# Dense matmuls issued in four 32-column tiles, and down weights loaded in the middle of the first GLU

## Chip, cores, metric

One core of one Trainium2 chip. The metric is the device time of one execution in microseconds; lower is better. Unless said otherwise, fast runs are compared with fast runs taken on the same chip in the same rounds. A "ratio" is the mean time of one kernel's fast runs over the mean of the other's fast runs of the same rounds, so it is not quite the ratio of the medians quoted beside it.

## The reference, cut

```python
def _A_ref(x, wqkv, wo):             # B=1, S=2048, D=640
    H = 32; Dh = 20; W = 256         # sliding window of 256 keys
    q, k, v = split_heads(x @ wqkv)
    scores = q k^T * Dh ** -0.5      # masked: 0 <= query - key < W
    p = softmax(scores)
    return merge_heads(p v) @ wo

def _B_ref(x, w_gate, w_up, w_down): # F=1536
    return (sigmoid(x @ w_gate) * (x @ w_up)) @ w_down

xn = layernorm(x)
return x + _A_ref(xn, wqkv, wo) + _B_ref(xn, w_gate, w_up, w_down)
```

All tensors are bf16.

## The kernel before

The sequence is cut into four chunks of 512 rows. A list of attention steps drives the order of TensorE's work: each of 76 steps computes scores, and two steps after a head group's last scores its PV (the product p v) follows (32 times). Between steps a queue of dense work ("fill": the GLU, which is `_B_ref` without its last product, projections, output) is emitted so that TensorE never waits for the exponential. All of it is unrolled: every matmul is an instruction pair, a weight load and a matmul (the trace of the kernel before has 4,666 loads and 4,631 matmuls).

```python
def proj_block(w, c, m):                       # q and k
    ...
        nc.tensor.matmul(ps, lhsT=wt[:, m, :], rhs=xnT[c][:, d, :],
                         start=(d == 0), stop=(d == DC - 1))        # 128x128 tile, 512 columns

def g_gu(c, f0, f1):                           # GLU, gate and up: the same form, 512 columns
def project_v / down / add_wo                  # the same form, 320 columns

def scores(c, step):
    ...                                        # four heads, 20 rows each, 64 columns: 20*64 tiles
        nc.tensor.matmul(ps[hf * U:(hf + 1) * U, i, ...],
                         lhsT=qk["k", kc][32 * i:32 * i + DH, g, key:key + U], rhs=qk["q", c][...])
def pv(c, g, parts):
    ...                                        # four heads side by side: 128*32 tiles
        nc.tensor.matmul(acc[32 * i:32 * i + 32, ...], lhsT=v[:, h * VW:h * VW + 32], rhs=pt[:, i, ...])

# the order of the steps
for t, (c, k, step) in enumerate(todo):
    ...
    for group in [x for x in ends if ends[x] == t - 2]:
        pv(*group, parts.pop(group))           # dense -> PV
    made = (step, scores(c, step))             # PV or dense -> scores
    ...
    credit = fill.pull(credit)                 # scores -> dense
```

q and k go through a scratch in DRAM to be spread over partitions; each chunk from the second on reads back 1 MB of q and 1 MB of k (in two pieces).

## Time and profile before

| | before |
|---|---|
| time, median (lowest to highest) | 315.97 us (315.47 to 316.91), 4 runs |
| TensorE instructions in the program | 9,334 |
| TensorE (PE) busy | 98% of the span, clock 1.0 |
| next busiest engine | ScalarE, 61% |
| drains (stops of TensorE at a change of tile size, about 95 ns each from the last tile's end) | 185, about 19.6 us |

PE is the bound; the prediction below shows the lines and how they are read. One line also belongs here. This is the queue on which PE's own instructions arrive (packets, MB, share of 16 engines' span):

```profile
q8 instruction: 36, 0.59, 0.8%
```

36 packets of 16 KB in 314 us: with 9,334 instructions of PE that is some 259 a packet.

### The profile page before, as it was taken

The page shows a single profiled execution, that of the slowest core. Times are in us where ns is not written, and L with a number is a line of the kernel's source. Part 1 is how long each engine was busy: PE and PEld are TensorE (multiplying, and loading weights), DVE is VectorE, ACT ScalarE, POOL GpSimd, SP SyncE. Part 2 cuts the span into 40 slices and gives each one's busy share as a digit, 9 for nine tenths or more (in the row PEclk, how much of TensorE's full clock was granted, in tenths as well). Part 3 has the DMA queues.
Part 4 walks back from the last instruction along what each step waited for, and adds up shares of the span by engine and source line. Part 5 has one row for each costly group of instructions (what it writes and reads, how often), then busy time and mean ns, then how long its engine had stood idle before and what let it go on. Part 6 is the DMA issues. An engine that isn't in the chain of part 4 may idle for free.

```text
span 314.3 us, 10536 instructions
## 1 busy us (share of the span) xinstructions
PE 306.9 (98%) x4631; PEld 176.7 (56%) x4666; DVE 157.3 (50%) x313; ACT 193.2 (61%) x179; POOL 159.8 (51%) x257
## 2 busy tenths in 40 slices
PE   8999999999999999999999999999999999999996
PEld 3654444456566656544566656544456664444674
DVE  3531486654855553447943542454552433673234
ACT  5723786788754468676644558776765657777200
POOL 3000487676768447454955536355355655565300
PEclk9999999999999999999999999999999999999999
DMA  7996976935823155500045025600000010000002
GB/s 237 376 319 195 322 189 121 369 139 187 225 59 70 41 180 190 172 4 0 2 47 85 23 103 154 205 3 2 3 2 23 23 44 2 4 2 2 1 2 83
DMA packets 34573, 33.08 MB, mean 105 GB/s; under 512 B 9920, under 2 KB 33984, under 8 KB 34496
## 3 DMA queue, kind: packets, MB, share of 16 engines
q1 hardware_dynamic: 34096, 32.14, 34.1%
q8 instruction: 36, 0.59, 0.8%
q10 hardware_dynamic: 432, 0.28, 0.3%
q14 instruction: 9, 0.07, 0.1%
HBM read 21.00 MB, written 10.26 MB: 99 GB/s over the span
## 4 chain that ended last, share of the span: by engine, by line
PE 85%; DMA 8%; SPq 2%; ACT 2%; issue 1%; DVE 0%; ACTq 0%
PE y L413 14%; PE pu L399 14%; PE pqk L292 13%; PE pg L392 13%; PE ps L459 7%; PE acc L491 7%; PE y L420 6%; PE pv L318 5%; DMA wu<-in_B_w_up_dram 4%; DMA sk<-st 3%; DMA wo<-wo_i 2%; PE pwarm L236 2%; PE d L413 2%; SPq L221 1%; ACT pT L464 1%
## 5 line engine op out<-in xcount | busy, mean ns | idle before, releaser
L467 POOL TENSOR_SCALAR_AFFINE_SELECT pT<-pT 128x512 bf16<-128x512 bf16 (+2 forms) x192 | 145.5, 789 | 132.8 <-ACT pT L464 132.7
L464 ACT ACTIVATE pT<-ps 128x2048 bf16<-128x2048 f32 x76 | 142.7, 1878 | 63.3 <-PE ps L459 60.5
L403 DVE SCALAR_TENSOR_TENSOR h<-th,pu 128x512 bf16<-128x512 f32 x48 | 32.9, 685 | 53.8 <-PE pu L399 29.2
L392 PE MATMUL pg<-xnT,wg 128*128 128x512 bf16 x226 | 58.9, 380 | 0.7
L399 PE MATMUL pu<-xnT,wu 128*128 128x512 bf16 x228 | 58.0, 380 | 1.3 <-issue 0.6
L413 PE MATMUL y<-wd,h 128*128 128x320 bf16 (+1 forms) x348 | 50.2, 297 | 0.0
L292 PE MATMUL pqk<-xnT,wqkv 128*128 128x512 bf16 x191 | 45.6, 381 | 0.5
L413 PEld LDWEIGHTS <-h 128*128 128x128 bf16 x396 | 36.7, 98 | 14.3
L501 DVE STREAM_TRANSPOSE t<-acc 128x512 f32<-128x512 f32 x32 | 22.8, 713 | 34.6 <-PE acc L491 34.3
L395 ACT ACTIVATE th<-pg 128x512 f32<-128x512 f32 x48 | 28.6, 595 | 17.8 <-PE pg L392 13.3
L399 PEld LDWEIGHTS <-wu 128*128 128x128 bf16 x240 | 22.0, 98 | 25.8 <-issue 0.6
L392 PEld LDWEIGHTS <-wg 128*128 128x128 bf16 x240 | 22.0, 98 | 25.1 <-issue 0.2
L459 PE MATMUL ps<-qT,kT 20*64 20x128 bf16 (+4 forms) x1856 | 32.5, 239 | 0.4 <-ACT pT L464 0.2
L292 PEld LDWEIGHTS <-wqkv 128*128 128x128 bf16 x200 | 22.5, 119 | 18.0 <-issue 0.6
L459 PEld LDWEIGHTS <-kT 20*64 20x64 bf16 x1856 | 20.7, 103 | 19.3 <-issue 16.0
L424 DVE SCALAR_TENSOR_TENSOR xn<-y,xc 128x320 bf16<-128x320 f32 (+1 forms) x29 | 13.9, 483 | 29.8 <-PE y L420 29.8
L491 PEld LDWEIGHTS <-v 128*32 128x32 bf16 x1376 | 19.5, 97 | 13.6 <-issue 11.0
L491 PE MATMUL acc<-pT,v 128*32 128x64 bf16 (+3 forms) x1376 | 26.0, 223 | 0.0
L318 PE MATMUL pv<-wqkv,xnT 128*128 128x320 bf16 x160 | 23.8, 300 | 0.2 <-DVE xnT L273 0.2
L513 DVE TENSOR_TENSOR on<-t,rec 128x320 bf16<-128x320 f32 (+4 forms) x48 | 22.2, 463 | 1.1
L420 PE MATMUL y<-wo,oc 128*128 128x320 bf16 (+1 forms) x145 | 21.6, 297 | 0.3 <-DMA wo<-wo_i 0.3
L296 DVE CAST st<-pqk 128x512 bf16<-128x512 f32 x20 | 13.7, 690 | 12.3 <-PE pqk L292 11.4
(49 smaller groups left out, 153.6 us busy)
## 6 DMA issues: line engine op xcount, KB each, us to landing
qT<-sq SPq DMA_DIRECT2D x3, 1024.0 KB, 6.0
sq<-st SPq DMA_DIRECT2D x20, 128.0 KB, 3.4
sk<-st SPq DMA_DIRECT2D x20, 128.0 KB, 4.2
out_dram<-xn SPq DMA_DIRECT2D x15, 160.0 KB, 1.8
kT<-sk SPq DMA_DIRECT2D x3, 768.0 KB, 5.7
wg<-in_B_w_gate_dram SPq DMA_DIRECT2D x2, 960.0 KB
wu<-in_B_w_up_dram SPq DMA_DIRECT2D x2, 960.0 KB, 11.3
xc<-in_A_x_dram SPq DMA_DIRECT2D x3, 640.0 KB, 5.0
```

The source lines that it names most:

```text
L292: nc.tensor.matmul(ps, lhsT=wt[:, m, :], rhs=xnT[c][:, d, :], start=(d == 0), stop=(d == DC - 1))
L318: nc.tensor.matmul(ps[:, 0:HALF], lhsT=xnT[c][:, d, s * P:(s + 1) * P], rhs=wqkv[:, d, 2 * D + hf * HALF:2 * D + (hf + 1) * HALF], start=( ...
L392: nc.tensor.matmul(pg, lhsT=part(wg, d, f), rhs=xnT[c][:, d, :], start=(d == 0), stop=(d == DC - 1))
L395: nc.scalar.activation(out=th, in_=pg, func=TANH, scale=0.5)
L399: nc.tensor.matmul(pu, lhsT=part(wu, d, f), rhs=xnT[c][:, d, :], start=(d == 0), stop=(d == DC - 1))
L403: nc.vector.scalar_tensor_tensor(out=h, in0=th, scalar=1.0, in1=pu, op0=ADD, op1=MULT)
L413: nc.tensor.matmul(y[:, 0:cut[1] - cut[0]], lhsT=ht[c, f][:, s * P:(s + 1) * P], rhs=wd[:, f, cut[0]:cut[1]], start=(f == 0), stop=False)
L420: nc.tensor.matmul(y[:, 0:cut[1] - cut[0]], lhsT=oc[c, m][:, s * P:(s + 1) * P], rhs=wo[:, m, cut[0]:cut[1]], start=False, stop=(m == DC - 1))
L459: nc.tensor.matmul(ps[hf * U:(hf + 1) * U, i, col * U:(col + n) * U], lhsT=qk["k", kc][32 * i:32 * i + DH, g, key:key + U], rhs=qk["q", c] ...
L464: nc.scalar.activation(out=pt[:, :, 0:CW], in_=ps, func=EXP, scale=SCALE)
L467: nc.gpsimd.affine_select(out=out, in_=in_, pattern=[[0, HG], [0, n], [sign, width]], compare_op=GE, fill=0.0, base=base, channel_multipli ...
L491: nc.tensor.matmul(acc[32 * i:32 * i + 32, q * U:(q + n) * U], lhsT=v[:, h * VW:h * VW + 32], rhs=pt[:, i, col * U:(col + n) * U], start=( ...
```

## The change

Its intent: PV works in 128*32 tiles, dense work in 128*128, and each change of tile size costs one of these drains of about 95 ns. If dense work uses 128*32 too, the drain between dense work and PV falls away. The down weights are loaded earlier, while the DMA engines have room.

```diff
+    def dense(out, lhsT, rhs, start, stop):
+        for j in range(0, P, 32):
+            nc.tensor.matmul(out[j:j + 32], lhsT=lhsT[:, j:j + 32], rhs=rhs, start=start, stop=stop)
...
-            nc.tensor.matmul(ps, lhsT=wt[:, m, :], rhs=xnT[c][:, d, :],
-                             start=(d == 0), stop=(d == DC - 1))
+            dense(ps, wt[:, m, :], xnT[c][:, d, :], d == 0, d == DC - 1)
 (the same for gate, up, down, wo, and for v of chunks 1 to 3)
...
-    fill.add("gu0", mix(g_gu(0, 0, 12), g_norms(1, True), 9), 12 * GU)
+    fill.add("gu0a", g_gu(0, 0, 4), 4 * GU)
+    fill.add("wd", later(load_wd), 0)
+    fill.add("gu0b", mix(g_gu(0, 4, 12), g_norms(1, True), 1), 8 * GU)
     fill.add("x2", later(load_x, 2), 0)
-    fill.add("wd", later(load_wd), 0)
```

More of the change, by code (lines that the diff above doesn't have):

```diff
@@ L317, in project_v @@
         for d in range(DC):
-            nc.tensor.matmul(ps[:, 0:HALF], lhsT=xnT[c][:, d, s * P:(s + 1) * P],
-                             rhs=wqkv[:, d, 2 * D + hf * HALF:2 * D + (hf + 1) * HALF],
-                             start=(d == 0), stop=(d == DC - 1))
+            (dense if c else nc.tensor.matmul)(
+                ps[:, 0:HALF], lhsT=xnT[c][:, d, s * P:(s + 1) * P],
+                rhs=wqkv[:, d, 2 * D + hf * HALF:2 * D + (hf + 1) * HALF],
+                start=(d == 0), stop=(d == DC - 1))
         return ps
@@ L391, in g_gu @@
             for d in range(DC):
-                nc.tensor.matmul(pg, lhsT=part(wg, d, f), rhs=xnT[c][:, d, :],
-                                 start=(d == 0), stop=(d == DC - 1))
+                dense(pg, part(wg, d, f), xnT[c][:, d, :], d == 0, d == DC - 1)
             th = tp.tile([P, CW], FP32, name="th")
@@ L398, in g_gu @@
             for d in range(DC):
-                nc.tensor.matmul(pu, lhsT=part(wu, d, f), rhs=xnT[c][:, d, :],
-                                 start=(d == 0), stop=(d == DC - 1))
+                dense(pu, part(wu, d, f), xnT[c][:, d, :], d == 0, d == DC - 1)
             h = hp.tile([P, CW], BF16, name="h")
@@ L412, in down @@
         for f in range(FC):
-            nc.tensor.matmul(y[:, 0:cut[1] - cut[0]], lhsT=ht[c, f][:, s * P:(s + 1) * P],
-                             rhs=wd[:, f, cut[0]:cut[1]], start=(f == 0), stop=False)
+            dense(y[:, 0:cut[1] - cut[0]], ht[c, f][:, s * P:(s + 1) * P],
+                  wd[:, f, cut[0]:cut[1]], f == 0, False)
             if f % 6 == 5:
@@ L419, in add_wo @@
         for m in range(DC):
-            nc.tensor.matmul(y[:, 0:cut[1] - cut[0]], lhsT=oc[c, m][:, s * P:(s + 1) * P],
-                             rhs=wo[:, m, cut[0]:cut[1]], start=False, stop=(m == DC - 1))
+            dense(y[:, 0:cut[1] - cut[0]], oc[c, m][:, s * P:(s + 1) * P],
+                  wo[:, m, cut[0]:cut[1]], False, m == DC - 1)
     def add_x(c, s, y, cut, rows):
```

## The prediction

> **What bounds the kernel now.** I read the page first, for the engine that sets the span.
>
> ```profile
> span 314.3 us, 10536 instructions
> PE 306.9 (98%) x4631; PEld 176.7 (56%) x4666; DVE 157.3 (50%) x313; ACT 193.2 (61%) x179; POOL 159.8 (51%) x257
> PEclk9999999999999999999999999999999999999999
> PE 85%; DMA 8%; SPq 2%; ACT 2%; issue 1%; DVE 0%; ACTq 0%
> ```
>
> TensorE matmuls (PE) cover 98% of the span at full clock, and PE makes up 85% of the chain that ended last; no other engine is above 61%. A matmul's recorded end is modelled, so 98% could still hide gaps. I therefore went to the PE's timeline and compared starts. This is one stretch of it, in the first output stage (start, length, what):
>
> ```profile
> 91.52 0.43 PE L459 MATMUL ps<-qT,kT 20*64 20x320 bf16 x24
> 91.88 2.62 PE L413 MATMUL y<-wd,h 128*128 128x320 bf16 x18
> 94.43 0.85 PE L491 MATMUL acc<-pT,v 128*32 128x320 bf16 x48
> 95.21 0.43 PE L459 MATMUL ps<-qT,kT 20*64 20x320 bf16 x24
> 95.57 1.53 PE L420 MATMUL y<-wo,oc 128*128 128x320 bf16 x10
> ```
>
> Three tile sizes alternate: 128*128 (dense), 128*32 (PV), 20*64 (scores, in 32-row by 64-column tiles). Inside a stretch there is no gap: 18 down matmuls are 2.62 us, the last one's modelled length is 0.30, so 17 spacings are 2.32 us, 136.5 ns each. At a change of size there is one. The last down matmul starts at 91.88 + 2.62 - 0.30 = 94.20 and should occupy the array to 94.34; PV begins at 94.43. Going through all starts of the trace in this way, with (columns / 2.4 + 3) ns for what a matmul or a set of concurrent tiles occupies (2.4 columns per ns is what 136 ns for 320 and 216 ns for 512 columns give), I find:
> - dense to PV: 32 changes, 96 ns each, 3.07 us in all;
> - PV to dense: 1 change, 108 ns;
> - dense to scores: 45 changes, 96 ns;
> - PV to scores: 31 changes, 107 ns;
> - scores to dense: 76 changes, 116 ns.
> The differences are the skew inside a concurrent set: its last tile starts about 12 ns (four PV tiles) or 23 ns (eight score tiles) after its first. Each change is then about 95 ns from the last tile. The sum is near 19.6 us. The first matmul after a change takes about 10 ns more than the next ones (146 against 136 ns). Outside the changes the remaining real stalls are few: some tenths of a us at 41.7, where PE waits for the second up weights, and at 89.25, where it waits for wo.
>
> ```profile
> 41.73 1.03 PE L399 MATMUL pu<-xnT,wu 128*128 128x512 bf16 x4 [0.32 <-DMA wu<-in_B_w_up_dram]
> 89.25 1.52 PE L420 MATMUL y<-wo,oc 128*128 128x320 bf16 x10 [0.25 <-DMA wo<-wo_i]
> ```
>
> So PE is bound by columns streamed plus changes of tile size. Only a change in those two, or a new wait, moves the time.
>
> [...] in the groups below a PV weight load takes 97 ns, as a dense one does (98), and it hides even under 64-column sets that start 28 ns apart.
>
> ```profile
> L491 PEld LDWEIGHTS <-v 128*32 128x32 bf16 x1376 | 19.5, 97 | 13.6 <-issue 11.0 <-DVE mv L250 0.4 <-DVE st L296 0.4
> L413 PEld LDWEIGHTS <-h 128*128 128x128 bf16 x396 | 36.7, 98 | 14.3
> L292 PEld LDWEIGHTS <-wqkv 128*128 128x128 bf16 x200 | 22.5, 119 | 18.0 <-issue 0.6
> ```
>
> [...] 2,000 successive PE instructions (1,000 load and matmul pairs) begin within 51.2 us, 51 ns a pair.
> [...] The trace shows the blocks (36 of them on the PE's instruction queue, about 1 us each)[...].
>
> **The change, part by part.**
> *Dense in four column tiles.* All gate, up, q, k, down and wo matmuls, and V of chunks 1 to 3, become four 128*32 ones with the same moving operand. The instruction lists agree: 17,500 PE rows against 9,334, so 8,166 more, which is 1,361 dense matmuls x 3 extra x 2 (load and matmul). Columns streamed stay the same if the four run side by side, as in PV: a 320-column PV set at 94.715 is followed by the next at 94.851, 136 ns, exactly a dense 320's. So the stream costs nothing more.
> - Removed: 32 dense-to-PV drains, 32 x 96 = 3.07 us; one PV-to-dense, 0.11; the slow first set after them, 32 x 10 = 0.32. Sum -3.50 us, all on PE, all on the path.
> - Added: before a score step the last dense set is now skewed by 11 ns, 45 x 11 = 0.50 us; one new change between the untiled V of chunk 0 and the q projection, 0.10 us. Sum +0.60.
> - Unchanged: the 76 changes into scores and the 76 out of them, since scores keep their own size. Some 16.4 of the 19.6 us of drains stay.
> Net -2.9 us, 0.9%.
>
> *Down weights earlier.* In the program's order the load now stands after four of twelve GLU blocks. It waits for no engine, so the queue issues it right behind the clears of the scratch, near 37.5 us in place of 52.4:
>
> ```profile
> 36.93 0.60 SPq L191 DMA_DIRECT2D sk<-kT  x1
> 44.77 6.92 SPq L276 DMA_TRANSPOSE xnT<-xn  x4
> 51.74 0.58 SPq L155 DMA_DIRECT2D xc<-in_A_x_dram  x1
> 52.38 0.63 SPq L212 DMA_DIRECT2D wd<-in_B_w_down_dram  x1
> ```
>
> The windows view tells what it meets: DMA share 0.99 from 36 to 43 us, 0.13 from 43 to 46, 0.84 from 46 to 53 (the transposes), 1.02 from 53 to 61 (x and wd). The load is 1.97 MB, at the 345 GB/s of the last window 5.7 us. It fills 43 to about 48.7, the idle stretch and the start of the transposes, which then end near 56 and not 53.7. The next projection needs them all at 56.9. So it is hidden, with under 1 us to spare; I allow +0.2 us. What it frees (the q stores that stood behind it at 60 to 66 us) was not on PE's path; gain 0. wd itself is first read near 82 us and was never late.
> A little of the gain may be lost at 89 us, where the wait for wo grows if PE arrives sooner: +0.1.
>
> Sum: 315.8 - 2.9 + 0.3 = 313.2 us.
>
> **The rivals.**
> 1. *Dispatch becomes the bound.* Dense 320-column work will need 8 instructions per 136 ns, 17 ns each, and the whole program averages about 300 us / 17,500 = 17 ns. PV and score bursts need 7 ns (144 instructions in 1.03 us)[...]. Against: PV and score bursts show no stall at their end[...]. So it is harmless or plainly harmful, with little between: about 318 to 325 us if it bites.
> 2. *Four column tiles don't stream side by side for dense operands.* All four read one moving operand, where PV's four read different ones, and the q and k weights are strided (119 ns a load against 98). For: no dense case is in the trace. Against: PV reads four streams at full rate, and 216 ns per 512-column set leaves room for loads. If the q and k sets alone lost 10%, that is 200 x 22 ns = 4.3 us, and the time 317.
> 3. *The early load collides.* If the transposes end after 57 us, PE waits at the first projection; at most the 2 to 3 us that they slip less the margin, so 314 to 315 us.
> 4. *The change saves more*, since dense to scores also gets cheaper between column-tiled sizes. Against: PV to scores costs 107 ns now, both column-tiled, no less than dense to scores.
>
> **Range and chances.** The arithmetic of the drains is firm to about 0.5 us: 312.6 to 313.6 if nothing else occurs. Rival 3 and a mild form of 1 or 2 stretch that to 317. A strong form of rival 1 gets 14%: slower by over 2% means above 322.1. Faster by over 2% means below 309.5, which would need another 3.7 us, more than the drains removed hold: 3%. I predict 313.2 us, 312.0 to 317.0 in eight of ten, 0.03 faster, 0.83 same, 0.14 slower.
>
> **What would show it.** Right: in the PE's timeline PV follows dense work without a gap (starts one set apart), the matmul sets of 320 and 512 columns keep 136 and 216 ns, changes into and out of scores keep 107 and 116 ns, and the GLU's first projection near 57 us shows no DMA wait. Rival 1: gaps of PE with "issue" as their reason, or sets that start more than 136 ns apart, most in the output stages and V, where sets have 320 columns, and least in the GLU. Rival 2: longer spacing at all shapes or at q and k only, GLU included. Rival 3: a wait of the q projection on the transposed xnT. I am wrong if the drain remains between dense and PV although both have 128*32, or if the 320-column sets come out above 140 ns in the output stages.

## The result, and the profile after

The changed kernel took 325.99 us (324.14 to 327.44, 4 runs) against 315.97: ratio 1.031, 95% interval 1.0247 to 1.0374. The fast runs of a second set on another occasion (after_again below) gave 1.031 too. It is slower by about 3%; the prediction was 313.2 us.

The page of the changed kernel, to be held against the first lines of the prediction and the instruction queue above:

```profile
span 325.0 us, 18737 instructions
PE 310.6 (96%) x8749; PEld 195.3 (60%) x8749; DVE 158.2 (49%) x313; ACT 193.4 (60%) x179; POOL 159.3 (49%) x257
PEclk9999999899999999999999999999999999999999
q8 instruction: 68, 1.11, 1.4%
```

PE is busy for 96% and no longer 98%, of a longer span; one slice shows a lower clock; and 68 blocks of instructions had to be fetched where 36 were (17,500 instructions in place of 9,334). No other engine became busier.

The intended effect is there. PE's timeline of the changed kernel around one PV (start, length, what, idle before and its end):

```profile
88.76 1.25 PE L284 MATMUL pu<-xnT,wu 128*32 128x512 bf16 x20
89.84 0.64 PE L494 MATMUL acc<-pT,v 128*32 128x320 bf16 x24
91.61 0.21 PE L494 MATMUL acc<-pT,v 128*32 128x64 bf16 x4 [1.13 <-issue]
91.76 0.43 PE L462 MATMUL ps<-qT,kT 20*64 20x320 bf16 x24
```

Five up sets of 216 ns begin at 88.76 and end at 89.84, and PV begins at 89.84: the drain is gone. Going through all starts, sets of four tiles keep the spacing of one dense matmul (about 3 ns over columns / 2.4: 136 ns for 320 columns, 216 for 512), changes into scores take 106 ns and out of scores 114 ns, as predicted. Set against the same sums of the kernel before, drains and first sets are 3.5 us less.

But the same lines show what came in: PV stops in the middle for 1.13 us, waiting for nothing that the profile knows ("issue"). In the table of waits of the changed kernel (engine, line, waited for: us in total, times, longest):

```profile
PE pv L284 <- issue: 2.9, 2, 2.1
PE pu L284 <- issue: 2.0, 1, 2.0
PE ps L462 <- DMA kT<-sk: 1.7, 1, 1.7
PE acc L494 <- issue: 1.1, 1, 1.1
```

I then listed every place after 14 us where a matmul starts over 60 ns later than the one before it and a drain explain, with the number of the instruction in PE's stream:

| start of the gap, us | gap, us | (instruction + 64) / 256 |
|---|---|---|
| 31.45 | 1.74 | 3.34 (the wait for kT) |
| 43.20 | 0.34 | 5.27 |
| 48.24 | 0.31 | 6.01 |
| 53.45 | 2.12 | 7.01 |
| 55.80 to 59.1 | 1.5 in all | 7.05 to 7.24 (half clock) |
| 90.26 | 1.30 | 14.01 |
| 94.88 | 0.14 | 15.01 |
| 102.16 | 0.71 | 17.00 |
| 110.29 | 0.48 | 19.00 |
| 123.19 | 0.24 | 22.00 |
| 136.23 | 0.92 | 25.00 |
| 186.67 | 0.39 | 37.01 |
| 208.49 | 2.29 | 42.01 |
| 81.30, 247.74, 261.75 | 0.07 each | 12.00, 50.00, 54.00 |

(Left out: three of under 0.1 us inside PV runs.) All gaps but three kinds (kT, the second up weights, half clock) fall on one place modulo 256: 64 instructions short of a multiple, as PE's instructions are counted here. 17,500 instructions over 68 packets are 257 each, and over 36 the 9,334 of the kernel before are 259, so I take 256 instructions for the size of a fetched block, and call these places boundaries. Where the constant 64 comes from is not shown. The gaps at boundaries sum to 9.1 us.

The DMA packets of the instruction queue tell the rest. In the trace PE's fetches start, where transfers are few, mostly within about 1.3 us of the moment at which PE comes to a boundary, and take 0.9 to 1.5 us. By their order (the 41st of the 68 starts at 208.47 us, before the gap at boundary 42) each brings the block that begins at the next boundary. The fetch before the gap at 208 us should by this rule have begun at 204.84 us. It began at 208.47, 3.6 us late, while the DMA engines were 94% busy in the 4 us before (the 1 MB of q came in), and ended at 209.36. PE began the last instruction that it had at 208.49 and the next at 210.91, 1.5 us after the end of the fetch. This is so at all nine boundary gaps of over 0.2 us in this trace: PE goes on 1.2 to 1.6 us after the packet of its block has ended (in the traces of after_again, tile_only, quiet_qk and shift84 too). So the end of a gap follows the fetch, and a block here must last longer than the fetch's lateness, its 0.9 to 1.5 us and these 1.2 to 1.6 us together. The fetch before the gap at 53 us was 5.2 us late, with the transposes and the down weights in flight. In the kernel before, fetches were up to 4.0 us late too (at 76 us). But there a block of 256 instructions lasted 5.7 us or more, mostly 7 to 9; now it mostly lasts 3.0 to 5.8. Lateness goes with traffic: of the changed kernel's fetches from the fourth on, the 16 that fell due with the DMA engines over 50% busy in the next 2 us were 2.4 us late in the median, the 33 with under 10% 0.4 us.

After the gap at 53 us the clock was cut. Timeline and windows of the changed kernel (the windows give, for each stretch, busy time and instructions of PE, PEld, DVE, ACT and POOL, then the granted clock, DMA share and GB/s):

```profile
52.57 1.26 PE L284 MATMUL pu<-xnT,wu 128*32 128x512 bf16 x18
55.78 0.61 PE L284 MATMUL pu<-xnT,wu 128*32 128x512 bf16 x2 [1.96 <-issue]
57.90 2.04 PE L284 MATMUL pu<-xnT,wu 128*32 128x512 bf16 x20
```

```profile
53.40:55.80 2.40, 0.44 (x11) 0.02 (x5) 1.82 (x4) 2.33 (x2) 0.76 (x1) 0.97 1.30 126
55.80:59.20 3.40, 3.40 (x36) 1.34 (x40) 0.69 (x1) 0.63 (x2) 1.94 (x3) 0.52 1.26 315
59.20:62.20 3.00, 3.00 (x94) 1.85 (x90) 2.06 (x4) 1.22 (x1) 0.00 (x0) 1.00 0.49 185
```

PE stands from 53.8 to 55.8; for the next 3.4 us the clock is 0.52 and a 512-column set takes 427 ns, not 216. This adds 1.5 us to the 2.1 us of that gap. Not every such stop is followed by half clock: after the gap at 208 us, where PE stands from 208.8 to 210.9, the windows from 211 to 217 us show a clock of 1.00, and the stop of 2.0 us at 53 us in after_again, a run with a mean clock of 1.0, was not followed by it either.

The sum: 314.3 us span before, less 3.5 of drains, plus 12.3 us of gaps that it did not have (9.1 at boundaries, 1.7 for kT, 1.5 at half clock; the 0.3 for the second up weights were there before), gives 323.1; the span is 325.0. About 2 us are left over: 0.3 of them come before my list begins (q's first projection starts at 14.36 us, before at 14.07), the rest I cannot name.

### The profile page after: what moved, and what is told of

The parts are those of the page before. It is cut to its first block, busy times and chain, and to the rows that moved or that the text cites. A ratio compares the mean times of both kernels' runs of the same rounds, so it can differ in the third digit from the quotient of the medians.

```text
span 325.0 us, 18737 instructions
## 1 busy us (share of the span) xinstructions
PE 310.6 (96%) x8749; PEld 195.3 (60%) x8749; DVE 158.2 (49%) x313; ACT 193.4 (60%) x179; POOL 159.3 (49%) x257
## 4 chain that ended last, share of the span: by engine, by line
PE 89%; DMA 5%; issue 3%; ACT 1%; SPq 1%; DVE 0%
PE y L284 21%; PE pg L284 15%; PE pu L284 15%; PE pqk L284 14%; PE ps L462 8%; PE acc L494 6%; PE pv L284 5%; DMA wu<-in_B_w_up_dram 3%; PE d L284 2%; PE pv L322 2%; DMA sk<-st 1%; DMA xc<-in_A_x_dram 1%; SPq L311 1%; PE acc L284 0%; PE pt L272 0%
## 5 line engine op out<-in xcount | busy, mean ns | idle before, releaser
L284 PE MATMUL pu<-xnT,wu 128*32 128x512 bf16 x960 | 62.1, 383 | 2.2 <-issue 2.0
L284 PE MATMUL pg<-xnT,wg 128*32 128x512 bf16 x960 | 62.4, 385 | 0.1
L284 PE MATMUL y<-wd,h 128*32 128x320 bf16 (+1 forms) x1392 | 50.8, 297 | 0.2 <-issue 0.2
L284 PEld LDWEIGHTS <-h 128*32 128x32 bf16 x1584 | 41.2, 97 | 10.4 <-issue 0.6
L284 PE MATMUL pqk<-xnT,wqkv 128*32 128x512 bf16 x800 | 46.6, 381 | 0.1
L284 PEld LDWEIGHTS <-wu 128*32 128x32 bf16 x960 | 25.3, 97 | 26.5 <-issue 4.4
L284 PEld LDWEIGHTS <-wg 128*32 128x32 bf16 x960 | 25.0, 97 | 23.8 <-issue 1.9
L284 PEld LDWEIGHTS <-wqkv 128*32 128x32 bf16 x800 | 24.0, 116 | 17.2 <-issue 1.2
L284 PE MATMUL y<-wo,oc 128*32 128x320 bf16 (+1 forms) x580 | 22.0, 297 | 0.0
L284 PE MATMUL pv<-wqkv,xnT 128*32 128x320 bf16 x480 | 18.4, 300 | 2.9 <-issue 2.9
```

Of the source, the lines that this page charges most:

```text
L284: nc.tensor.matmul(out[j:j + 32], lhsT=lhsT[:, j:j + 32], rhs=rhs, start=start, stop=stop)
```

## The experiments

Theory 1: PE runs out of fetched instructions. The stream is twice as dense, so a block lasts half as long, and a fetch that waits among bulk transfers comes too late. Rivals: a fixed rate of dispatch per instruction (rival 1 as predicted); a cost of column tiling itself; the moved load alone.

**wd_only.** The load moved, dense matmuls untouched.

```diff
 (kernel before)
-    fill.add("gu0", mix(g_gu(0, 0, 12), g_norms(1, True), 9), 12 * GU)
+    gu0a, wd, gu0b, x2 in the order of the change
```

> The kernel before with the down weights loaded in the middle of the first GLU, dense matmuls untouched. Theory 1 (instruction supply: PE runs out of fetched 256-instruction blocks because the stream is twice as dense and the block fetch waits behind bulk transfers): no effect, 315.2 to 316.6 us. Rival 3 (the early load collides with the transposes and PE waits at the first projection): 317 to 319 us, with a wait of the q projection near 57 us.

Measured: 315.55 us (315.19 to 316.51, 20 runs), before 316.25; ratio 0.9977 (0.9969 to 0.9984). The moved load alone does no harm. It gains 0.7 us where I expected none. Why is not shown. Of the two small waits of the kernel before, that of scores for the exponential at 69 us (0.21 us) is gone, and that for wo at 89 us is 0.08 us in place of 0.25, which is 0.4 us together; but the profiled spans differ by 0.1 us only (314.2 and 314.3).

**tile_only.** The tiling without the moved load.

```diff
 (changed kernel)
-    gu0a, wd, gu0b, x2
+    gu0, x2, wd as before
```

> The changed kernel with the down weights loaded where they were before. Theory 1: still slow, 321 to 327 us; PE gaps again begin at a 256-instruction boundary of the PE stream, and the 2 us gap at 53 us shrinks or moves to where the load now is (55 to 63 us). Rival 3 (the moved load makes the loss): 313 to 314 us, the drains' gain.

Measured: 324.10 us (322.77 to 324.89); ratio 1.0242 (1.0211 to 1.0272). The tiling makes most of the loss. The gap of 2.1 us at 53 us, with its half clock, is gone, and others stand at boundaries 9, 12 and 13 instead (0.9, 0.5, 0.2 us); that at boundary 14 stays (1.6 us, in the changed kernel 1.3). Rival 3 alone falls. But with tiling the moved load seems to cost some 2 us, where it gained 0.7 without: the fast runs of the changed kernel's two sets gave 1.031 against 1.0242 here, though not in the same rounds.

**pre_pv.** The drain can only be saved where dense work ends in a PV: 32 of the 77 dense stretches. The other 45 end in scores, with a drain either way. So only the former, and the tail, are tiled.

```diff
+    tiled = [False]
     def dense(out, lhsT, rhs, start, stop):
+        if not tiled[0]:
+            nc.tensor.matmul(out, lhsT=lhsT, rhs=rhs, start=start, stop=stop)
+            return
 ...
+        tiled[0] = any(e == t - 1 for e in ends.values())   # after the scores of step t
 ...
+    tiled[0] = True                                          # tail
 (down weights loaded as before)
```

> Only the dense work between a score step and the PV that follows it is issued in four column tiles (that is where the drain is saved), and the tail; the down weights load as before. 12,988 PE instructions in place of 17,500 (before: 9,334). Theory 1: the 3 us of drains are saved all the same, blocks of 256 instructions last longer, so few of the gaps stay: 313 to 318 us. A fixed dispatch rate per instruction as the bound: the tiled stretches slow as in the changed kernel, about half its loss, 319 to 322 us.

Measured: 314.50 us (313.65 to 315.02); ratio 0.994 (0.9917 to 0.9963), correct. With 12,988 instructions in place of 17,500 the result turns from 3% slower to 0.6% faster, though every dense-to-PV drain is saved. In its profile one gap of some tenths of a us stands at a boundary (308.5 us, 0.3), and one of 0.8 us is of another kind:

```profile
69.27 0.42 PE L466 MATMUL ps<-qT,kT 20*64 20x320 bf16 x16 [0.84 <-ACT pT L471]
```

Scores wait for an exponential that came late. Just before, ScalarE had stood idle for 2.05 us ahead of a copy of q or k; the profile puts this down to VectorE. That a store held the copy's buffer, as the expectation of pre_pv_wd below says, is not shown.

**quiet_qk.** A wrong result on purpose: same PE instructions, less traffic from the third chunk's projections on.

```diff
 (changed kernel)
 def proj_block(w, c, m):
 ...
+        if c >= 2:
+            return                     # no store to the scratch
 def spread(w, c, g0, g1):
+        if c >= 2:
+            qk[w, c] = qk[w, c - 1]    # chunk 1's q and k again
+            return
```

> Wrong result on purpose: the changed kernel, but chunks 2 and 3 take their q and k from chunk 1, so the stores to the scratch and the 1 MB and 768 KB loads back fall away from about 110 us on; PE's instructions are the same 17,500. Theory 1: the gaps at 110, 123, 136, 186 and 208 us (0.5, 0.2, 0.9, 0.4, 2.3 us) go, 320 to 323 us. Dispatch rate as the bound: no gap goes, 325 to 327 us.

Measured: 325.91 us (322.59 to 326.75); ratio 1.027. By the total this is a miss. The part before the edit takes effect differs from run to run: its profiled run met gaps of 2.5 us at 31 and 2.7 us at 55 us, each followed by 3.4 us of half clock, where the changed kernel's had one such event. What the edit can change is the stretch between instructions 5,700 and 10,800 of PE's stream. It took 82.9 us, and 86.8 in the changed kernel's run. About the same stretch in the windows view (81 matmuls more in the first), quiet_qk first, then the changed kernel:

```profile
128.00:218.00 90.00, 90.00 (x2766) 57.85 (x2762) 45.15 (x91) 59.63 (x56) 51.22 (x84) 1.00 0.08 19
```

```profile
124.50:217.00 92.50, 89.40 (x2685) 58.03 (x2681) 44.08 (x89) 59.49 (x54) 49.91 (x82) 1.00 0.29 86
```

With 8% DMA share PE has no idle time at all; with 29% it stands for 3.1 us. Here is the place of the gap at 208 us, the changed kernel first:

```profile
207.85 0.43 PE L462 MATMUL ps<-qT,kT 20*64 20x128 bf16 x32
208.21 0.58 PE L284 MATMUL pv<-wqkv,xnT 128*32 128x320 bf16 x9
210.91 1.27 PE L284 MATMUL pv<-wqkv,xnT 128*32 128x320 bf16 x31 [2.12 <-issue]
```

```profile
210.00 0.43 PE L467 MATMUL ps<-qT,kT 20*64 20x128 bf16 x32
210.36 1.54 PE L284 MATMUL pv<-wqkv,xnT 128*32 128x320 bf16 x40
```

The same 40 matmuls run through. The two fetches concerned, 3.6 and 5.5 us late in the changed kernel, are 0.7 and 0.6 us late here. The instructions and their rate of dispatch are the same, so a fixed rate per instruction is not what stops PE. Of the five gaps that the expectation named, the last three are gone. The first two stay, at 0.2 and 0.3 us: the one at 113.6 us comes before the first store that was taken away (near 118 us in the changed kernel), and the one at 126.8 us behind a fetch that was 2.5 us late, while the load of x, which is still there, kept the DMA engines 82% busy.

**shift84.** 84 more PE instructions ahead of all work, to move every boundary.

```diff
 (tile_only)
-    for n in (7, 6):
+    for n, w in ((7, CW), (2, CW), (46, 8)):
         ps = ps_d.tile(...)
         for k in range(n):
-            nc.tensor.matmul(ps, lhsT=warm[:, 0:P], rhs=warm, ...)
+            nc.tensor.matmul(ps[:, 0:w], lhsT=warm[:, 0:P], rhs=warm[:, 0:w], ...)
```

> tile_only with the last four of the warm-up matmuls replaced by 46 of 8 columns: 84 PE instructions more ahead of all work, so that every boundary of 256 instructions falls 84 instructions earlier in the work. Theory 1: the gaps stay at multiples of 256 counted from the start of the stream, so they come before other instructions of the work than in tile_only; time 322 to 326 us. Rival (the gaps belong to places in the work, a hidden wait on a buffer or a transfer): they stay before the same instructions of the work, 84 rows later in the stream.

Measured: one run of 330.06 us, of unknown state, above what I expected; one of its gaps was followed by half clock, and a stretch of half clock near 9 us comes behind the small warm-up matmuls that my edit put in. What it was for is where the gaps are. Besides three near the wait for kT and the up weights, (instruction + 64) / 256 is 9.00, 10.00, 13.00, 15.01, 17.00, 18.00, 20.00, 25.00, 38.02, 42.01, 52.00, 54.00 and 55.00. The gap at boundary 9, in tile_only first, then in shift84:

```profile
62.61 0.67 PE L494 MATMUL acc<-pT,v 128*32 128x320 bf16 x28
63.21 0.43 PE L462 MATMUL ps<-qT,kT 20*64 20x320 bf16 x24
63.57 0.85 PE L284 MATMUL pqk<-xnT,wqkv 128*32 128x512 bf16 x12
65.15 1.72 PE L284 MATMUL pqk<-xnT,wqkv 128*32 128x512 bf16 x28 [0.73 <-issue]
```

```profile
62.23 0.64 PE L494 MATMUL acc<-pT,v 128*32 128x320 bf16 x22
63.95 0.26 PE L494 MATMUL acc<-pT,v 128*32 128x128 bf16 x6 [1.08 <-issue]
64.14 0.43 PE L462 MATMUL ps<-qT,kT 20*64 20x320 bf16 x24
64.50 0.85 PE L284 MATMUL pqk<-xnT,wqkv 128*32 128x512 bf16 x12
```

In shift84 the stop comes before 6 PV, 24 score and 12 projection matmuls that in tile_only are ahead of it: 42 pairs, 84 instructions. The gap went with the boundary, not with the work. A wait on a buffer or a transfer of the work would have stayed with the work.

**from_c2.** Full tiling, but only once the steps of chunk 2 begin.

```diff
 (tile_only, with the switch of pre_pv)
+        tiled[0] = c >= 2              # after the scores of each step
```

> Full tiling, but only once the steps of chunk 2 begin; down weights as before. 13,954 PE instructions. About half of the PVs keep their drain (16 x 0.1 us saved, 0.2 us added by skew). Theory 1: bulk transfers are few there except q and k of chunk 3 near 200 to 215 us, so the gaps are at most the 2.9 us that the changed kernel had after 180 us, and none before: 314.5 to 317.5 us. A cost of column tiling itself, per matmul: half of the changed kernel's loss, 319 to 321 us.

Measured: 319.19 us over all 16 runs (316.56 to 323.76), of which four are slow by the rule of 1.5% over the fastest; the 12 fast ones have a median of 318.2 us, ratio 1.0059 (1.0035 to 1.0083). The fast runs lie above the range of theory 1 and below that of the rival, and the median of all 16 at the lower end of the rival's; it does not decide. The profile fell in a slow run (323.8 us). In it one gap of 2.7 us at 202 us stands at a boundary whose fetch was 3.8 us late, followed by half clock; but another 2.2 us, at 85 us, is a wait of scores for k in a stretch that is not tiled at all. Why that wait came, and what puts the fast runs 1.9 us above the kernel before, is open.

**after_again** (the changed kernel, unedited) and **split_q** (the 1 MB load of q cut in four):

```diff
 (changed kernel)
-                if w == "k" and m == 1:
-                    spread("q", c, 0, NG if c else 2)
+                if w == "k" and c and m > 0:
+                    spread("q", c, 2 * m - 2, 2 * m)
+                if w == "k" and m == 1 and c == 0:
+                    spread("q", c, 0, 2)
```

> The changed kernel once more, as it is, for comparison on the same chip: 323 to 328 us.

> The changed kernel with the 1 MB load of q (chunks 1 to 3) cut into four of 256 KB, one behind each of the last four stores of k, so that no long run of packets stands ahead of an instruction fetch. Theory 1 with the fetch waiting behind bulk packets: the gaps near 79 to 95, 136 and 208 us shrink, 1.5 to 4 us off the changed kernel's time. If the fetch is late for another reason than queued packets: within 1 us of the changed kernel.

Measured: after_again 326.77 us over all four runs (324.22 to 329.12). The longest is slow; the three fast ones have a median of 325.79 us and a ratio of 1.031. (The ratio on record, 1.0365, fits the three unprofiled runs, the slow one among them.) split_q 329.25 us (328.44 to 332.0), ratio 1.0434 (1.0397 to 1.0472). The cut did not help, and the result is outside both expectations: over 3 us slower. At the places that it concerns, split_q still has gaps at boundaries 13, 14, 25 and 42 of 0.5, 1.9, 0.9 and 1.1 us; after_again has 0.2, 1.6, 0.6 and 0.7. Three of the four fetches in question are 2.2 to 4.8 us late in split_q. So taking the traffic away lets fetches come in time (quiet_qk); spreading the same bytes did not. Split_q also met three stretches of half clock (at 35, 59 and 96 us), two of them before its edit takes effect, in a build where all four runs had a mean clock of 0.984 to 0.989. Each follows a gap of 1.9 us or more (2.2, 3.1 and 1.9). Why this build meets more of them I cannot explain.

**pre_pv_wd** and **pre_pv_wd_q.** pre_pv with the moved load; and with the cut load as well.

```diff
 (pre_pv)
-    gu0, x2, wd as before
+    gu0a, wd, gu0b, x2 in the order of the change
 (pre_pv_wd_q: and the diff of split_q)
```

> Tiling only in the stretches that end in a PV, as in pre_pv, and the down weights loaded in the middle of the first GLU, as in wd_only. Theory 1: both gains add, and the 0.84 us gap near 69 us (scores waiting for the exponential, which waits behind a copy of q or k whose buffer a store held) shrinks: 313.0 to 314.0 us, 0.8% below the kernel before. If the moved load costs what it did in the fully tiled kernel (2 us): 316 us.

> pre_pv_wd with the same cut of the q load. Theory 1: blocks last over 5 us there and few fetches come too late, so little is left to win: 312.3 to 313.3 us (0.988 to 0.991 of before). If late landings of the stores still cost there: 311.5 to 312.3.

Measured: pre_pv_wd 313.02 us (312.19 to 313.80, 5 runs), ratio 0.9902 (0.9882 to 0.9921), correct. pre_pv_wd_q 313.50 us (312.65 to 314.33), ratio 0.9922, just above the range expected: the cut brings nothing. The first beats both kernels of this study: 1.0% under the kernel before, some 4% under the changed one. PE's timeline of pre_pv_wd at the place that the prediction showed first, and its instruction queue:

```profile
91.19 2.63 PE L288 MATMUL y<-wd,h 128*32 128x320 bf16 x72
93.65 0.84 PE L498 MATMUL acc<-pT,v 128*32 128x320 bf16 x48
94.42 0.43 PE L466 MATMUL ps<-qT,kT 20*64 20x320 bf16 x24
94.78 1.53 PE L285 MATMUL y<-wo,oc 128*128 128x320 bf16 x10
```

```profile
q8 instruction: 50, 0.82, 1.1%
```

18 sets of 136.5 ns begin at 91.19 and end at 93.65, where PV begins. Then, from scores to scores, dense work is 128*128 again. 50 blocks are fetched, and "issue" holds PE up for tenths of a us only.

## Why the prediction was wrong, point by point

- *PE is the bound, in columns streamed plus changes of tile size.* Right for the kernel before. It left out a third resource of PE's, the supply of instructions, which was not the bound yet. All the signs that the prediction listed for being right are there (no drain before PV, sets of 136 and 216 ns, changes of 106 and 114 ns, no wait of q's projection on a DMA); none of them looks at the supply.
- *32 drains of 96 ns fall away; net 2.9 us.* Right in mechanism and nearly in size: about 3.5 us by the starts in the changed kernel's trace. pre_pv_wd gained 3.1 us in all, of which the moved load is perhaps 0.7.
- *Streaming costs no more in four tiles; weight loads stay hidden.* Right: 136 and 216 ns a set in every variant at full clock. Rival 2 is refuted by the same spacing.
- *Rival 1, the instruction rate.* This step failed. I treated the supply as a rate per instruction, and asked whether 17 ns was enough. In the changed kernel's trace 1,000 successive PE instructions begin within 12.9 us, under 13 ns each where 17 were needed: the rate was ample. I saw the block packets ("36 of them, about 1 us each") and did not take the next step: how long a block lasts, and how late its fetch can be. The numbers were there in the trace of the kernel before: fetches up to 4.0 us late in heavy traffic, blocks of mostly 7 to 9 us. Halving the block's time to 3 to 5.8 us brings the two together: with the 0.9 to 1.5 us of the fetch and the 1.2 to 1.6 us after it, a lateness of 2 us is already too much for many blocks. The term that I set to 0 in the sum was 9.1 us at boundaries in the profiled run, plus 1.5 us of half clock.
- *"Harmless or plainly harmful", 14%.* The signature that I named for rival 1 (gaps of PE with "issue") is what came, and the time I gave to it (318 to 325 us) is near. That it is near is luck: it was my estimate, reckoned from a rate per instruction that no trace had shown and that is not the cause. The chance was too low, and the place half wrong: I expected V and output stages; the costliest gap, with its half clock, was in a GLU stage, where the block before it had lasted 5.2 us (48.24 to 53.45), near the upper end of the 3.0 to 5.8, but the DMA engines were busy throughout (a share of 1.20 to 1.30 from 50 to 59.2 us).
- *The moved load is hidden, +0.2 us.* Alone it gains 0.7 us (wd_only), of which two shorter waits on PE's path explain 0.4 at most. In the fully tiled kernel it puts its 1.97 MB and the transposes around the fetch that is needed at boundary 7, and a gap of 2.1 to 3.1 us stands there in all four profiles with the move (changed kernel, after_again, quiet_qk, split_q); in the two without it (tile_only, shift84) there is none. The ratios (1.031 with it, 1.0242 without) suggest a cost of some 2 us, not measured in one set of rounds.
- *Range.* 312.0 to 317.0 held the drains' arithmetic and mild forms of the rivals, and gave the third resource no room.

Shown: the gaps sit on 256-instruction boundaries and move with them (shift84); they end 1.2 to 1.6 us after the fetch of the block; less traffic at the same instructions removes them (quiet_qk, in its stretch); fewer instructions with the same drains saved remove nearly all of them (pre_pv). Not shown: why the fetches are late by the amounts that they are. They come later in traffic (2.4 us in the median with the DMA engines over 50% busy, 0.4 with under 10%), but cutting the largest load did not help. Nor is traffic needed for a small gap: in the output stages, where a block can last 3.0 us, after_again stands for 0.4 us at 251 us and again at 259, with the DMA engines at most 2% busy, and shift84 for 0.9 us at 262 us with 8%. Also open is the wait for kT at 31 us (1.7 us). It comes in the profiled runs of the changed kernel, tile_only, quiet_qk and split_q, and at 0.5 us in shift84's, but not in that of after_again, which is the same program as the changed kernel. In the changed kernel's trace the last packets of the store of k pass right after an instruction fetch of 0.9 us; whether fetches hold up data as well, no run tests.

## What to carry to other kernels

Where PE's work is fully unrolled, count instructions per microsecond, and hold the time that a block of 256 lasts (here 7 to 9 us before, 3 to 5.8 after) against how late fetches already come in the busiest DMA stretch, plus the 2 to 3 us that the fetch itself and the start after it took here. Gaps of PE that wait for nothing and lie multiples of 256 instructions apart pointed to missing fetches here; the packets of PE's instruction queue, which ended 1.2 to 1.6 us before PE went on, told. And when a finer tiling saves a drain, use it only in the stretches that end in that drain: that saved every one of these drains here for 45% of the added instructions (pre_pv, ratio 0.994, where full tiling gave 1.0242).
